# Attention into SwiGLU on one core: three more warming products and a paced one on TensorE, and v of batch 3 loaded in four steps from ScalarE's queue

## The chip, the cores and the metric

The kernel runs on one core of a Trainium2 chip. The metric is device microseconds of one execution. Before the change the median of 4 runs is 328.59 us (328.45 to 328.79).

## The reference

The inputs are q, k and v of shape (8 batches, 8 heads, 576 positions, 64), three weights and a gain of a feed-forward block, and the output is (4608, 512) float32. Each batch first goes through a linear attention with a positional weight, and every token then through a normalised SwiGLU block:

```
phi(x)  = concat(relu(x) * cos_w, relu(x) * sin_w)            # 64 -> 128 features
kv, z   = sum_s phi(k)[s] v[s]^T,  sum_s phi(k)[s]            # per head
attn    = phi(q) kv / (phi(q) . z + 1e-6)
x       = attn, heads side by side: (4608 tokens, 512)
xn      = x / sqrt(mean(x^2) + 1e-6) * rms_g
out     = (silu(xn w_gate) * (xn w_val)) w_out                # 512 -> 1536 -> 512
```

## The kernel before, in words

Every instruction is placed by hand; each engine runs its own list in order, and a semaphore makes one list wait for another. The names below are those of the code.

**A batch's attention.** `load_kv` and `load_q` (issued from SP, the sync engine) bring raw k, v and q into the tiles rk, rv and rq. There are two rk tiles, but only one rv and one rq. `k_phi` and `q_phi` (lines 209 on ScalarE, 211 on VectorE) make the cos half and the sin half of phi, in bf16, in kpm and qp. `v_cast` (line 265 on VectorE, 263 on ScalarE) makes vvm, v in bf16 with a column of ones; there are two vvm tiles. `kvz_pe` (72 small products, line 282, PSUM tile psA) sums phi(k) with v, first for the heads of the low half (pieces 0 and 1), then for the high half. `kvz_evac` copies the sum out. phi(q) is transposed by a DMA (`q_tr_dma`, line 246). `nd_pe` (line 310, psA again, for each of four groups j of 128 tokens) multiplies it with the sum; `nd_post` (lines 360 to 364, VectorE: rec, then xt) divides, and so frees psA for the next group; `x_sq` (line 375, ScalarE: scr) squares and sums; GpSimd takes the power -1/2 (rs, line 380); `x_norm` (line 387, VectorE: xn) scales; `x_tr_dma` (line 406) transposes into xnT. The last 64 positions of two batches share a fifth group (qtT, xnt_tail).

**A block of the feed-forward part.** Block b works on the first 512 positions of batch b, in slots. In slots 0 to 11 `gval_step` runs eight 128x512 products (line 426, into psG and psV, each with two banks used in turn), ScalarE takes the silu (line 435, sg) and VectorE multiplies (line 441, hT). In slots 12 to 15 `out_step` runs the twelve products of an output tile (line 446, psC), ScalarE copies it out (line 263, osb) and issues its store. Attention work of the next batch is hung into the slots: "pe" stands ahead of a slot's products, "pre" and "post" ahead of and behind its evacuation, and "mid" lies between the sixth and the seventh product of an output slot.

In block 1, attention of batch 2 is under way: the groups j = 0 to 3 have their `nd_pe` in slots 7, 9, 11 and in the middle of slot 12. Loads of batch 3 are issued there too:

```
n = (p, 13, 6 + p)[i] if b == 1 else 5 * i + p
at(b + n // 16, n % 16, "post", load_piece, which, nb, p)
```

For nb = 3 (b = 1) this puts piece p of k in slot p, all four pieces of v in slot 13, and piece p of q in slot 6 + p. In later batches the pieces of v are spread over slots 5 to 8. The two halves of v of batch 3 are cast by VectorE in block 2, in slot 1 (low) and slot 3 (high), behind that slot's `q_phi`; `kvz_pe` of batch 3 stands at the head of slot 4.

**Completion semaphores.** The loads, stores and transposes that SP and ScalarE issue share eight completion semaphores, which are handed out in turn in the order of the code over both queues. An instruction that issues a transfer waits until the transfer that had its semaphore before has landed, and what stands behind it on its engine waits as well.

**The opening.** While k of batch 0 arrives, TensorE runs products of a zero tile (`filler`, line 466). Behind twelve of them stand three `paced` products: each takes a slice of kpm as its weights, so it waits for that slice (`paced(7, 1)` for group 7 of the low half; `paced(0, 3)` and `paced(5, 3)` for groups of the high half), and each has one more filler behind it. Between the second and the third lies the product that spreads the gain over the partitions (line 487). Then follow the transposes of phi(q) (line 254).

Of the kernel before, what the change touches and what calls it, by code (L numbers as in the profile page):

```python
# [23 lines left out]
def kernel(  # L24
# [11 lines left out]
    nc = tc.nc  # L36
# [28 lines left out]
    NJ = 9  # L65
# [2 lines left out]

    raw = {}

    def load_kv(which, b, r0=0, r1=4, j0=0, j1=NJ):

        key = (which, b)
        if key not in raw:
            raw[key] = (two if which == "k" else one).tile(
                [P, 4, NJ * D], FP32, name=f"r{which}", tag=f"r{which}"
            )
        src = {"k": k, "v": v}[which]
        return nc.sync.dma_start(
            out=raw[key][:, r0:r1, j0 * D : j1 * D],  # L80
            in_=src[b, 2 * r0 : 2 * r1, :, :]
            .rearrange("h s d -> (h s d)")
            .rearrange("(r p n) -> p r n", p=P, n=NJ * D)[:, :, j0 * D : j1 * D],
        )

    def load_q(b, h0=0, h1=8):
        key = ("q", b)
        if key not in raw:
            raw[key] = one.tile([P, H, 4 * D], FP32, name="rq", tag="rq")
        return nc.sync.dma_start(  # L90
            out=raw[key][:, h0:h1, :],
            in_=q[b, h0:h1, 0:512, :].rearrange("h (p j) d -> p h (j d)", j=4),
        )

    def load_q_tail(b):
        t = four.tile([P, 4, D], FP32, name="rqt", tag="rqt")
        raw[("qt", b)] = t
        for g in range(2):
            d = nc.sync.dma_start(
                out=t[64 * g : 64 * g + 64, :, :],  # L100
                in_=q[b, 4 * g : 4 * g + 4, 512:576, :].rearrange("h s d -> s h d"),
            )
        return d

    def load_piece(which, b, p):
        if which != "q":
            load_kv(which, b, p, p + 1)
        elif p < 4:
            load_q(b, 2 * p, 2 * p + 2)
        else:  # L110
            load_q_tail(b)
# [12 lines left out]
    g_row = one.tile([1, DM], FP32, name="g_row")  # L124
    nc.scalar.dma_start(out=g_row[:, :], in_=moe_rms_g.rearrange("(o d) -> o d", o=1))
    load_kv("k", 0, *LOW)
    load_kv("k", 0, *HIGH)
    load_q_tokens(0, 0, 2)
    first_v = load_kv("v", 0, *LOW)
# [334 lines left out]
    def filler(n, bank):  # L464
        for _ in range(n):
            nc.tensor.matmul(bank, lhsT=warm[:, 0:P], rhs=warm[:, :], start=True, stop=True)


    idle = psO[1][:, :]
# [4 lines left out]
        for j in range(NJ):  # L474
            k_phi(A if rs is LOW or j < 6 else V, 0, j, 1, rs)

    def paced(j, r):

        nc.tensor.matmul(
            idle, lhsT=kp_main[0][:, j, r, :], rhs=warm[:, :], start=True, stop=True  # L480
        )
        filler(1, idle)

    filler(12, idle)
    paced(7, 1)
    paced(0, 3)
    nc.tensor.matmul(psG[0][:, :], lhsT=ones[:, :], rhs=g_row[:, :], start=True, stop=True)
    paced(5, 3)
    weight_dmas = []

    def gval_slice(c0, c1):
# [145 lines left out]
    def at(blk, n, where, f, *args):  # L637
        slots.setdefault((blk, n), none())[where].append((f, args))
# [26 lines left out]
    for nb in range(2, B):  # L665
        b = nb - 1
# [24 lines left out]
        for j in range(4):  # L691
            n = nds[j]
# [12 lines left out]
    for nb in range(3, B):  # L705

        b = nb - 2
        for i, which in enumerate(("k", "v", "q")):
            for p in range(5 if which == "q" else 4):
                n = (p, 13, 6 + p)[i] if b == 1 else 5 * i + p  # L710
                at(b + n // 16, n % 16, "post", load_piece, which, nb, p)

    def gval_step(blk, n, bank=None):
# [31 lines left out]
    for n in range(NNT - 2):  # L745
# [28 lines left out]
        if n in nd_at:  # L774
            j = nd_at[n]
# [52 lines left out]
    for (c0, c1), bank in (((0, 384), psC[1]), ((384, 512), psG[0])):  # L828
# [6 lines left out]
        for i in range(2):  # L835
            r0 = (6 + i) * S + 512
# [33 lines left out]
```

## Time and profile before

| | before |
|---|---|
| median of 4 runs | 328.59 us |
| the profiled execution: its time, its span | 328.45 us, 326.7 us |
| TensorE busy | 317.7 us (97%), 2441 products |
| VectorE, ScalarE, GpSimd busy | 185.5 us, 177.6 us, 32.0 us |
| granted TensorE clock, mean | 0.999 |
| bytes moved by DMA | 53.91 MB, mean 165 GB/s |

The span is the time from the first to the last instruction; 1.75 us of the run lie outside it. In the timelines a row gives its start, its duration, the engine, the line, the operation and how many were merged; the bracket at the end is the idle time of that engine just before it, and what ended it. PEld is the loading of weights on TensorE, ACT is ScalarE, DVE is VectorE, and a q behind an engine's name marks the issuing of a DMA on it.

### The profile page before, as it was taken

Reading aid. Unit: us, or ns where it says so; the run is one execution under the profiler, and the core shown is the slowest. Engines: PE = TensorE matmul, PEld = TensorE weight load, DVE = VectorE, ACT = ScalarE, POOL = GpSimd, SP = SyncE. Lnnn points to the kernel's source line nnn. Section 1 sums busy time; section 2 is a strip of 40 time slices with the busy share of each in tenths; the row PEclk is TensorE's granted clock in tenths of the full one; section 3 lists DMA queues with packets and bytes.
Section 4 is the critical chain, followed back from the end, with each engine's and each line's share of the span. In section 5 each row is a group of like instructions: output and inputs, shape, how many; then the busy total and the mean of one; then the engine's idle time right before and its main releaser. Section 6 shows DMA issues by size and latency. Waiting matters only on the chain.

```text
span 326.7 us, 6421 instructions
## 1 busy us (share of the span) xinstructions
PE 317.7 (97%) x2441; PEld 161.0 (49%) x2441; DVE 185.5 (57%) x412; ACT 177.6 (54%) x366; POOL 32.0 (10%) x67
## 2 busy tenths in 40 slices
PE   7999999999998999999999999999999999999994
PEld 2587465555444444554454445444544444444442
DVE  6875758777765766578257745773577133203310
ACT  6963865964774457644754476547644333223321
POOL 1660112001000100010001100110011000000000
PEclk9999999999999999999999999999999999999999
DMA  7999999999699665976597669957621400020014
GB/s 270 232 196 267 316 165 323 321 189 224 125 239 267 176 191 154 205 211 178 166 222 203 167 199 206 201 148 222 122 41 32 130 32 0 32 99 1 0 34 97
DMA packets 80338, 53.91 MB, mean 165 GB/s; under 512 B 51377, under 2 KB 67761, under 8 KB 80306
## 3 DMA queue, kind: packets, MB, share of 16 engines
q1 hardware_dynamic: 68752, 40.52, 50.6%
q0 software_dynamic: 6880, 4.72, 10.1%
q10 hardware_dynamic: 4674, 8.26, 7.7%
q8 instruction: 19, 0.31, 0.4%
q14 instruction: 13, 0.11, 0.1%
HBM read 37.75 MB, written 9.44 MB: 144 GB/s over the span
## 4 chain that ended last, share of the span: by engine, by line
PE 90%; DVE 4%; ACT 2%; DMA 1%; issue 1%; ACTq 0%; DVEq 0%
PE psG L426 26%; PE psC L446 26%; PE psV L426 26%; PE psA L282 3%; PE psA L310 2%; PE psG L446 1%; DVE kpm L211 1%; PE psG L565 1%; DMA rk<-in_k_dram 1%; PE psV L565 1%; PE psO L565 1%; DVE vvm L265 1%; DVE qp L211 1%; ACT kpm L209 1%; PE psC L830 1%
## 5 line engine op out<-in xcount | busy, mean ns | idle before, releaser
L441 DVE TENSOR_TENSOR hT<-psV,sg 128x512 bf16<-128x512 f32 x102 | 70.3, 689 | 93.1 <-PE psV L426 82.0
L435 ACT ACTIVATE sg<-psG 128x512 f32<-128x512 f32 x102 | 60.6, 594 | 64.9 <-PE psG L426 64.8
L426 PE MATMUL psG<-xnT,wg 128*128 128x512 bf16 (+1 forms) x368 | 92.9, 375 | 0.1
L426 PE MATMUL psV<-xnT,wv 128*128 128x512 bf16 (+1 forms) x368 | 92.7, 374 | 0.0
L446 PE MATMUL psC<-wo,hT 128*128 128x512 bf16 x396 | 89.5, 379 | 0.0
L426 PEld LDWEIGHTS <-wv 128*128 128x128 bf16 x416 | 40.7, 98 | 47.3
L446 PEld LDWEIGHTS <-hT 128*128 128x128 bf16 x420 | 40.2, 98 | 46.7
L426 PEld LDWEIGHTS <-wg 128*128 128x128 bf16 x416 | 38.5, 98 | 41.0 <-DVE xnT L265 0.4
L380 POOL TENSOR_TENSOR rs<-ms,mhalf 128x1 f32<-128x1 f32 x36 | 19.8, 549 | 200.9 <-ACT scr L375 200.9
L387 DVE SCALAR_TENSOR_TENSOR xn<-xt,rs,gb 128x512 bf16<-128x512 f32 x36 | 26.8, 745 | 19.3 <-POOL rs L380 19.3
L263 ACT COPY osb<-psC 128x512 f32<-128x512 f32 (+1 forms) x33 | 19.1, 579 | 32.5 <-PE psC L446 31.1
L375 ACT ACTIVATE scr<-xt 128x513 bf16<-128x513 f32 x36 | 22.8, 634 | 24.2 <-DVE xt L364 22.6
L209 ACT ACTIVATE kpm<-rk,tab 128x256 bf16<-128x256 f32 (+1 forms) x78 | 31.9, 476 | 7.0 <-ACT osb L263 5.4
L364 DVE TENSOR_TENSOR xt<-psA,rec 128x512 f32<-128x512 f32 x35 | 24.2, 691 | 1.2
L211 DVE TENSOR_SCALAR kpm<-rk,tab 128x256 bf16<-128x256 f32 (+1 forms) x84 | 22.2, 330 | 2.1 <-DMA rk<-in_k_dram 2.1
L209 ACT ACTIVATE qp<-rq,tab 128x512 bf16<-128x512 f32 x32 | 22.4, 713 | 0.0
L211 DVE TENSOR_SCALAR qp<-rq,tab 128x512 bf16<-128x512 f32 x32 | 15.1, 485 | 0.0
L310 PEld LDWEIGHTS <-qpT 128*128 128x128 bf16 x248 | 11.6, 98 | 6.7 <-issue 0.3
L310 PE MATMUL psA<-kvzs,qpT 128*128 128x65 bf16 x248 | 12.8, 194 | 0.2
L426 PE MATMUL psV<-xnt_tail,wv 128*128 128x512 bf16 x48 | 12.3, 379 | 0.0
L426 PE MATMUL psG<-xnt_tail,wg 128*128 128x512 bf16 x48 | 12.3, 379 | 0.0
L282 PEld LDWEIGHTS <-kpm 64*128 64x128 bf16 x576 | 9.9, 94 | 4.7 <-issue 4.0
(89 smaller groups left out, 167.5 us busy)
## 6 DMA issues: line engine op xcount, KB each, us to landing
out_dram<-osb ACTq DMA_DIRECT2D x28, 256.0 KB, 3.2
rv<-in_v_dram SPq DMA_DIRECT2D x21, 288.0 KB, 3.1
rk<-in_k_dram SPq DMA_DIRECT2D x20, 288.0 KB, 4.2
rq<-in_q_dram SPq DMA_DIRECT2D x20, 256.0 KB, 3.5
rk<-in_k_dram SPq DMA_DIRECT2D x2, 1152.0 KB, 8.8
rq<-in_q_dram SPq DMA_DIRECT2D x2, 1024.0 KB, 9.4
rv<-in_v_dram SPq DMA_DIRECT2D x3, 576.0 KB, 9.2
wo<-in_moe_w_out_dram POOLq DMA_DIRECT2D x4, 384.0 KB, 7.7
```

What stands on the lines that cost most here:

```text
L209: nc.scalar.activation(out=out_ap, in_=in_ap, func=AF.Relu, scale=scale)
L211: eng.tensor_scalar(out=out_ap, in0=in_ap, scalar1=scale, scalar2=0.0, op0=ALU.mult, op1=ALU.max)
L282: nc.tensor.matmul(banks[c][:, r * E : (r + 1) * E], lhsT=kp_main[b][lo : lo + 64, j, r, :], rhs=vvm[b % 2][lo : lo + 64, r, j, :], start= ...
L310: nc.tensor.matmul(o[:, g, i, :], lhsT=qpT[(b, 0)][:, h, j * P : (j + 1) * P], rhs=kvz_of(b, h), start=True, stop=True,)
L364: nc.vector.tensor_tensor(out=xt[:, 0:DM].rearrange("p (b h d) -> p b h d", b=2, d=D), in0=o[:, :, :, 0:D], in1=rec[:, :, :].unsqueeze(3). ...
L375: nc.scalar.activation(out=scr[:, :], in_=xt[:, 0 : DM + 1], func=AF.Square, scale=1.0 / math.sqrt(DM), accum_out=ms[:, :],)
L380: nc.gpsimd.tensor_tensor(out=rs[:, :], in0=ms[:, :], in1=mhalf[:, :], op=ALU.pow)
L387: nc.vector.scalar_tensor_tensor(out=xn[:, :], in0=x_of[(b, j)][:, 0:DM], scalar=rs_of[(b, j)][:, :], in1=gb[:, :], op0=ALU.mult, op1=ALU. ...
L426: nc.tensor.matmul(pst[bank][:, cols[0] : cols[1]], lhsT=w[:, t, n * P : (n + 1) * P], rhs=x[:, t, cols[0] : cols[1]], start=(t == 0), sto ...
L435: nc.scalar.activation(out=sg[:, :], in_=psG[bank][:, :], func=AF.Silu)
L441: nc.vector.tensor_tensor(out=hTs[blk][:, n, :], in0=psV[bank][:, :], in1=sg[:, :], op=ALU.mult)
L446: nc.tensor.matmul(bank, lhsT=hTs[blk][:, n, j * P : (j + 1) * P], rhs=wo[:, n, :], start=(n == 0), stop=(n == NNT - 1),)
```

## The change

There are two parts, in stages that lie some 70 us apart.

In the opening, fifteen fillers run in place of twelve; a fourth paced product, `paced(3, 1)`, which waits for group 3 of the low half of phi(k), stands ahead of the other three, with a filler behind it; and the filler behind the last paced product is gone. That is a net four products more.

In block 1, the four pieces of v of batch 3 are issued by ScalarE in place of SP, one each in slots 7, 8, 9 and 10, in place of all four in slot 13. The casts that read them stay where they are.

```
-    def load_kv(which, b, r0=0, r1=4, j0=0, j1=NJ):
+    def load_kv(which, b, r0=0, r1=4, j0=0, j1=NJ, eng=nc.sync):
...
-        return nc.sync.dma_start(
+        return eng.dma_start(
...
-            load_kv(which, b, p, p + 1)
+            eng = nc.scalar if (which, b) == ("v", 3) else nc.sync
+            load_kv(which, b, p, p + 1, eng=eng)
...
-    def paced(j, r):
+    def paced(j, r, more=1):
...
-        filler(1, idle)
+        filler(more, idle)
...
-    filler(12, idle)
+    filler(15, idle)
+    paced(3, 1)
     paced(7, 1)
     paced(0, 3)
     nc.tensor.matmul(psG[0][:, :], lhsT=ones[:, :], rhs=g_row[:, :], start=True, stop=True)
-    paced(5, 3)
+    paced(5, 3, 0)
...
-                n = (p, 13, 6 + p)[i] if b == 1 else 5 * i + p
+                n = (p, 7 + p, 6 + p)[i] if b == 1 else 5 * i + p
```

In the order in which the changed kernel is built, ScalarE's list in slots 7 to 11 of block 1 reads: x_sq (slot 7), **v piece 0**, phi of a tail, sg (slot 8), **v piece 1**, phi of a tail, sg (slot 9), x_sq (slot 9), **v piece 2**, sg (slot 10), **v piece 3**, sg (slot 11), x_sq (slot 11). VectorE's and GpSimd's lists have the same order as before. SP's list lacks the four v pieces and is otherwise in the same order. By the eight semaphores in turn, v piece 0 and v piece 1 each wait for a piece of k of batch 3, v piece 2 for piece 1 of q of batch 3, and v piece 3 for v piece 0.

## The prediction

> **What bounds the kernel now.** I read the page first (busy times, then the chain that ended last), then TensorE's waits, then the timelines of the two stages that the change touches.
>
> ```profile
> PE 317.7 (97%) x2441; PEld 161.0 (49%) x2441; DVE 185.5 (57%) x412; ACT 177.6 (54%) x366; POOL 32.0 (10%) x67
> PE 90%; DVE 4%; ACT 2%; DMA 1%; issue 1%; ACTq 0%; DVEq 0%
> ```
>
> TensorE is busy for 97% of the span and holds 90% of the last chain. A change gains only where TensorE idles, and whatever makes TensorE idle is lost one for one. Its waits:
>
> ```profile
> PE psA L282 <- DVE vvm L265: 1.2, 1, 1.2
> PE psO L466 <- DVE warm L145: 1.2, 1, 1.2
> PE psO L479 <- ACT kpm L209: 1.1, 1, 1.1
> PE psG L565 <- DVE xnT L265: 0.5, 1, 0.5
> PE psO L254 <- ACT qp L209: 0.3, 1, 0.3
> ```
>
> Two of these rows are near the change: 1.1 us ahead of the first paced product, and 1.2 us ahead of the high half of batch 3's sum, which waits for the cast of v.
>
> **Part 1, the opening: 0.** The weight loads, then the two products that matter:
>
> ```profile
> 4.58 0.15 PEld L466 LDWEIGHTS <-warm 128*128 128x128 bf16 x1 [0.28 <-issue]
> 4.98 0.31 PEld L466 LDWEIGHTS <-warm 128*128 128x128 bf16 x2 [0.25 <-issue]
> 6.92 0.10 PEld L479 LDWEIGHTS <-kpm 128*128 128x128 bf16 x1 [1.63 <-ACT kpm L209]
> 9.58 0.50 PEld L254 LDWEIGHTS <-qp 128*128 128x128 bf16 x9 [0.37 <-ACT qp L209]
> ```
>
> Up to 4.58 us a product takes 0.43 us; from 4.98 us on the spacing halves (7.73 - 7.51 = 0.22 between two later products). Twelve fillers end at 5.78 us. Five more products come ahead of `paced(7, 1)`: three fillers and the new pair, 5 x 0.22 = 1.1 us, against 1.14 us of idleness. The new paced product doesn't wait: ScalarE's fifteen phi steps take 4.49 us from 4.42, so its fourth ends at about 4.42 + 4 x 0.30 = 5.6 us, and VectorE's fourth of 21 (4.21 us from 4.44) at 5.2; TensorE gets there at about 6.2. `paced(7, 1)` therefore still starts at 6.92 us, when its own slice is there. The dropped filler frees 0.22 us ahead of the transposes, but these start at 9.58 us because phi of q ends on ScalarE at 8.82 + 0.70 = 9.52 us. So the work is covered from both sides: value 0. If the cover were gone, the four net products would cost 4 x 0.22 = 0.9 us; below nothing it can't go, since no later product in the opening waits for TensorE's own past: its waits of 0.3 and 0.5 us there are for ScalarE and VectorE. Nor can the pace improve: it is full from 5 us on (the granted clock reads 1.00 in the slow stretch too, so the spacing is the evidence).
>
> The Trainium skill speaks against this part ("TensorE: Matmul & The Clock Gate", Part 1): the half-rate start lasts until one whole free-running window of about 3.4 us was busy, so its end varies by run. By that rule an unlucky run would do all 17 products at 0.43 us and end them near 8.5 us, about 1.5 us late. The trace shows one run, with the change of pace at 5 us.
>
> The trace's own bound for a late change of pace: four runs lie within 0.34 us, so the pace can't wander much, and a rate change up to 6 us is absorbed (eleven of the 17 products done by then, six at 0.22 us end at 7.3 us, and the chain has 0.3 us to spare ahead of the transposes).
>
> **Part 2, v of batch 3: what it could gain is nothing.** The 1.2 us is not a wait for the transfer. In the chain of waits:
>
> ```profile
> 97.38 0.10 DVE hT L441
> ...
> 97.99 0.48 DVE qp L211
> 98.47 0.68 DVE vvm L265
> ...
> 99.19 0.76 PE psA L282 x36
> ```
>
> VectorE casts the high half only behind hT of slot 3, which waits for TensorE's last product of that slot, and behind a `q_phi`. There is no idle time between the three, and no wait for a DMA: the casts at 94.93 and 98.38 us start when VectorE is free. The order of VectorE's list is unchanged, so hT + phi + cast less the low half of the sum comes out at 1.2 us again. On SP, what stood behind the four v pieces is the tail's transpose at 92.18 us, and this waited for xn (91.40 + 0.75), not for the queue: 0.
>
> **What part 2 can cost** is on ScalarE. In the timelines (ScalarE, VectorE, TensorE; block 1, slots 9 to 12):
>
> ```profile
> 76.50 0.64 ACT L375 ACTIVATE scr<-xt 128x513 bf16<-128x513 f32 x1 [1.09 <-DVE xt L364]
> 77.13 0.58 ACT L435 ACTIVATE sg<-psG 128x512 f32<-128x512 f32 x1
> ```
>
> ```profile
> 77.74 0.69 DVE L441 TENSOR_TENSOR hT<-psV,sg 128x512 bf16<-128x512 f32 x1 [0.76 <-ACT sg L435]
> ...
> 79.44 0.69 DVE L364 TENSOR_TENSOR xt<-psA,rec 128x512 f32<-128x512 f32 x1
> ```
>
> ```profile
> 80.41 0.41 PE L310 MATMUL psA<-kvzs,qpT 128*128 128x65 bf16 x8
> ```
>
> This is a chain without slack. sg of slot 10 follows x_sq at once; hT waits for sg (0.76 us idle); xn, rec and xt run behind hT without a gap; xt frees psA at 79.44 + 0.69 = 80.13 us; and TensorE, in order, wants psA at 80.41 us. So 0.28 us, say 0.25 with the handover, is all that a delay D of sg may take; TensorE idles for D - 0.25.
>
> Pieces 0, 1 and 3 matter less: piece 1 stands ahead of an sg that waited 0.71 us, piece 3 behind the sg in question. Piece 0 delays hT of slot 8, and through VectorE's unbroken run from 73.74 to 76.99 us the x_sq of slot 9, by 0 to 0.43. Piece 2 stands directly between that x_sq and sg, and waits for q piece 1:
>
> ```profile
> 73.08 1.09 SPq L90 DMA_DIRECT2D rq<-in_q_dram  x2
> DMA to landing us min/median/max: 3.0/3.2/3.5
> ```
>
> (the second answer is of the tile rq in this stretch). q piece 1 is issued at about 73.65 us; landing by its row of 3.4 us: 77.05 us.
>
> Prices: issuing a v piece took 0.43 us (median of the four on SP near 87 us, 0.74 at most; stores of 256 KB on ScalarE 0.34 to 0.40): I take 0.43. No row shows whether ScalarE issues while its previous activation still runs, so both ends stand. Contention: v pieces now run beside q; one piece of 288 KB at the 287 GB/s of 73.3 to 74.2 us is 1.0 us.
> - Issue under the running activation, no contention: issue ends at 77.05 + 0.43 = 77.5, D = 0.4, stall 0.1.
> - Issue after it, no contention: piece 0 shifts x_sq to 76.93, with its accumulator read it ends near 77.65; issue to 78.1; D = 0.95, stall 0.7.
> - Contention, either way: q lands at 78.05, issue to 78.5; D = 1.35, stall 1.1.
>
> The first is one end; the other is a q piece that lands like the slowest v piece near 87 us (7.7 us): 81.35 + 0.43, D = 4.6, stall 4.4, which I hold for remote, since q rows here stay within 3.5. Counting the contended price once for each way of issuing, the four mean 0.75; I take **0.7 us**.
>
> By the Trainium skill ("DMA: Bandwidth & Descriptors", Issuing engines are not separate DMA queues) transfers from both queues interleave on the same 16 engines, so the second queue saves issue time alone; by it the contended price, 1.1 us, would stand.
>
> Downstream the shift runs along: x_sq, rs, xn and the transpose of group 3 (issued near 85.7 us, 4.1 us to landing: 89.8) move with TensorE, whose use is at 90.2 us.
>
> **Sum.** 0 + 0 + 0.7. The profiled execution took 328.45 us (span 326.7, 1.75 outside): 329.15. The median lies 0.14 us above it: **329.3 us**. A measurement of this kernel can't tell a difference within about 0.2%, 0.66 us, from none: that bound is 327.9 to 329.25.
>
> **The rivals.**
> - *Stall as reckoned*, 328.9 to 329.9 us: 0.5. Two thirds of it lie above 329.25.
> - *All of it hidden*: sg isn't held for more than 0.4 us; 328.4 to 328.9 us: 0.25. For it: ScalarE is 54% busy and idles 0.7 to 1.1 us before most sg. Against it: not before this one.
> - *q piece 1 lands late*, stall 1.5 to 3 us: 330.1 to 331.6 us, 0.1.
> - *The half-rate start lasts past 6 us*, and the longer warm-up delays the transposes: up to 0.9 us, 329.3 to 329.6 us with the stall small: 0.07.
> - *Faster*: the landing of v, not VectorE's order, holds the cast (the pieces took 5.4 to 7.7 us, so the last, issued at 88.7 us, landed as late as 96.4 us); landed earlier, it lets the cast go ahead and the wait of 1.2 us is gone: 327.4 us, 0.08. It decides only if the cast stood idle for the DMA, that is with a landing behind 98.4 us; in the trace VectorE has no such idle time.
>
> Slower: two thirds of 0.5, and 0.1, and most of 0.07, about 0.48; faster 0.08; the rest, 0.44, within the bound. The range leaves out the faster case and the late landing, 0.18: 328.3 to 330.0 us.
>
> **What would show it.** In the profile after: `paced(7, 1)` at 6.92 us with no idle time before it; the transposes at 9.58; ScalarE's third v issue at 77 to 78 us with sg behind it at 77.5 to 78.5; a new wait of TensorE's L310 for VectorE's xt near 80.4 us, of about 0.7; the 1.2 us ahead of L282 unchanged. No wait at L310 would prove the second case; an L282 wait that is gone would prove me wrong on VectorE's order; an L254 start after 9.6 us, on the opening.

## The result and the profile after

| | before | after |
|---|---|---|
| median of the runs shown with the result | 328.76 us (71 runs) | 329.98 us (45 runs) |
| ratio to before, 95% interval | | 1.0033 (1.0026 to 1.0039) |
| profiled execution: time, span | 328.45, 326.7 us | 329.88, 328.1 us |
| granted TensorE clock | 0.999 | 1.00 |

The change makes the kernel slower by 0.85 to 1.28 us. (Between the two profiled executions it is 1.43 us.) The page after, its busy times and the shares of the last chain by engine:

```profile
PE 318.5 (97%) x2445; PEld 161.4 (49%) x2445; DVE 185.8 (57%) x412; ACT 177.8 (54%) x366; POOL 31.9 (10%) x67
PE 87%; DMA 4%; DVE 3%; ACT 2%; issue 1%; SPq 1%; ACTq 0%; DVEq 0%
```

TensorE has its four products more. Its share of the last chain fell by 3 points, and transfers have more of it (DMA 4%, from 1%). About 1% is a load of q of batch 3, 4.37 us long, which nobody waited for before; most of the rest is a load of v in the opening, which landed later in this execution. Line numbers are one or two higher than before (L310 is L311, L435 is L436). TensorE's waits (total, times, longest) name the place:

```profile
PE psA L283 <- DVE vvm L266: 1.2, 1, 1.2
PE psO L467 <- DVE warm L146: 1.2, 1, 1.2
PE psA L311 <- DVE xt L365: 1.1, 1, 1.1
PE psG L567 <- DVE xnT L266: 0.5, 1, 0.5
PE psO L480 <- ACT kpm L210: 0.5, 1, 0.5
PE psO L255 <- ACT qp L210: 0.3, 1, 0.3
```

The third row is new. The 1.2 us ahead of the high half of batch 3's sum (first row) is still there. The wait ahead of the first paced products (L480) went from 1.1 to 0.5 us, but it was filled with products that nothing needs, so nothing was gained. ScalarE's timeline in slots 7 to 10 of block 1 shows where the third row comes from:

```profile
72.24 0.64 ACT L376 ACTIVATE scr<-xt 128x513 bf16<-128x513 f32 x1 [0.45 <-DVE xt L365]
72.37 0.38 ACTq L79 DMA_DIRECT2D rv<-in_v_dram  x1
...
76.64 0.64 ACT L376 ACTIVATE scr<-xt 128x513 bf16<-128x513 f32 x1 [1.09 <-DVE xt L365]
77.18 0.19 ACT L376 ACTIVATION_READ_ACCUMULATOR scr<-xt 128x1 f32 x1
78.37 0.36 ACTq L79 DMA_DIRECT2D rv<-in_v_dram  x1
78.78 0.60 ACT L436 ACTIVATE sg<-psG 128x512 f32<-128x512 f32 x1 [1.41 <-PE psG L427]
```

The third v piece is issued at 78.37 us, 1.00 us after the accumulator was read (77.18 + 0.19), and sg of slot 10, which followed at once before, starts behind it: 1.41 us of idleness. The bracket names psG as releaser, but psG had been full long before (its last product ended at 76.59 us): what came last is the issue, and what the issue waited for is piece 1 of q. The chain of waits in this stretch shows it (first block; "issue" is time without a wait that the profile shows). The second block is the answer for the tile rq, all four pieces of q:

```profile
73.98 4.37 DMA rq<-in_q_dram
78.35 0.02 issue
78.37 0.36 ACTq L79
```

```profile
DMA to landing us min/median/max: 4.2/4.3/5.3
```

Piece 1 of q, issued at 73.98 us, lands at 78.35 us, and the issue of v starts 0.02 us later. From there the chain runs through VectorE to TensorE:

```profile
79.40 0.69 DVE L442 TENSOR_TENSOR hT<-psV,sg 128x512 bf16<-128x512 f32 x1 [2.28 <-ACT sg L436]
...
81.10 0.69 DVE L365 TENSOR_TENSOR xt<-psA,rec 128x512 f32<-128x512 f32 x1
```

```profile
81.84 0.40 PE L311 MATMUL psA<-kvzs,qpT 128*128 128x65 bf16 x8 [1.13 <-DVE xt L365]
```

Before, TensorE needed 10.66 us from nd_pe of slot 7 (69.75) to nd_pe in the middle of slot 12 (80.41). After, it needs 11.95 us (69.89 to 81.84): 1.29 us more. From there to the first product of block 2 both need 9.79 us. The other 0.14 us were lost ahead of slot 7: in this execution v of batch 0 landed a little later. 1.29 + 0.14 = 1.43 us, the whole difference of the two profiles.

### The profile page after: what moved, and what is told of

It is laid out like the page before. It is cut to its first block, busy times and chain, and to the rows that moved or that the text cites. A ratio compares the mean times of both kernels' runs of the same rounds, so it can differ in the third digit from the quotient of the medians.

```text
span 328.1 us, 6430 instructions
## 1 busy us (share of the span) xinstructions
PE 318.5 (97%) x2445; PEld 161.4 (49%) x2445; DVE 185.8 (57%) x412; ACT 177.8 (54%) x366; POOL 31.9 (10%) x67
## 4 chain that ended last, share of the span: by engine, by line
PE 87%; DMA 4%; DVE 3%; ACT 2%; issue 1%; SPq 1%; ACTq 0%; DVEq 0%
PE psC L447 26%; PE psG L427 25%; PE psV L427 24%; PE psA L283 3%; DMA rv<-in_v_dram 2%; PE psA L311 2%; PE psG L447 1%; DMA rq<-in_q_dram 1%; PE psG L567 1%; PE psV L567 1%; PE psO L567 1%; ACT sg L436 1%; ACT kpm L210 1%; DVE xt L365 1%; PE psC L832 1%
## 5 line engine op out<-in xcount | busy, mean ns | idle before, releaser
L436 ACT ACTIVATE sg<-psG 128x512 f32<-128x512 f32 x102 | 60.6, 594 | 65.5 <-PE psG L427 65.4
L311 PEld LDWEIGHTS <-qpT 128*128 128x128 bf16 x248 | 11.6, 98 | 8.0 <-issue 1.7
L311 PE MATMUL psA<-kvzs,qpT 128*128 128x65 bf16 x248 | 12.8, 193 | 1.4 <-DVE xt L365 1.1
L283 PEld LDWEIGHTS <-kpm 64*128 64x128 bf16 x576 | 10.0, 95 | 4.9 <-issue 4.0
```

Of the source, the lines that this page charges most:

```text
L283: nc.tensor.matmul(banks[c][:, r * E : (r + 1) * E], lhsT=kp_main[b][lo : lo + 64, j, r, :], rhs=vvm[b % 2][lo : lo + 64, r, j, :], start= ...
L311: nc.tensor.matmul(o[:, g, i, :], lhsT=qpT[(b, 0)][:, h, j * P : (j + 1) * P], rhs=kvz_of(b, h), start=True, stop=True,)
L436: nc.scalar.activation(out=sg[:, :], in_=psG[bank][:, :], func=AF.Silu)
```

## The experiments

Two measures serve for all of them, both counted from nd_pe of slot 7 in the same execution, so that the opening drops out. D is how much later than before sg of slot 10 starts (before: 77.13 - 69.75 = 7.38 us). The loss is what the stretch from slot 7 to the middle of slot 12 exceeds 10.66 us by.

**The opening alone.** v stays with SP in slot 13.

```
-    filler(12, idle)
+    filler(15, idle)
+    paced(3, 1)
...
-    paced(5, 3)
+    paced(5, 3, 0)
```

> Only the opening is changed (fifteen fillers, the new paced product, no filler behind the last); v of batch 3 is loaded as before. Theory (the whole loss is the stall of TensorE at L310 behind ScalarE's third v issue): same time as before within 0.15% (0.5 us), the transposes of phi(q) at 9.6 us, no wait at L310. Rival (the opening costs something: the sum of phi(k) v of batch 0 began 0.14 us later in the profile after): 0.14 us slower or more, and that shift seen again near 10.8 us.

Measured: 328.83 us, ratio 0.9983 (0.9961 to 1.0005), loss 0.01 us. In the profiled execution the weight loads kept their slow spacing until 6.29 us, and still the transposes of phi(q) waited for ScalarE:

```profile
5.86 0.15 PEld L467 LDWEIGHTS <-warm 128*128 128x128 bf16 x1 [0.28 <-issue]
6.29 0.39 PEld L467 LDWEIGHTS <-warm 128*128 128x128 bf16 x2 [0.28 <-issue]
...
9.89 1.01 PEld L255 LDWEIGHTS <-qp 128*128 128x128 bf16 x16 [0.34 <-ACT qp L210]
```

So the opening costs nothing, and a late change of pace was absorbed: TensorE worked without a gap until the gain's product at 8.40 us, and was done in time. (ScalarE's phi of q was itself 0.3 us later here, as q of batch 0 landed at 9.1 us.) The rival's sign was there, and larger than expected: the sum of phi(k) v of batch 0 began at 11.37 us, 0.75 us later than before (10.62), and nd_pe of slot 7 as much later. It waited for the cast of v of batch 0, which landed 8.3 us after its issue, before 7.3. This isn't the opening's doing: with the old opening (next run) that landing took 8.6 us, with the new one (last run) 7.2.

**The load of v alone.** The opening stays as before; against the kernel after:

```
-    filler(15, idle)
-    paced(3, 1)
+    filler(12, idle)
...
-    paced(5, 3, 0)
+    paced(5, 3)
```

> Only the loading of v of batch 3 is changed. Theory: all of the change's loss, about +1.1 us (+0.33%), with a wait at L310 of about 1.1 us near 81.8 us. Rival (part of the loss is in the opening): +0.7 us or less.

Measured: 329.99 us, ratio 1.0023 (1.0005 to 1.0041), D 1.15 us, loss 0.94 us. The opening's part of the change is absent, and the wait is there. (The interval of the time alone, 0.2 to 1.3 us, doesn't tell the theory from the rival; the loss in the profile does.) TensorE's wait, then ScalarE's timeline:

```profile
PE psA L311 <- DVE xt L365: 0.8, 1, 0.8
```

```profile
78.96 0.36 ACTq L79 DMA_DIRECT2D rv<-in_v_dram  x1
79.37 0.60 ACT L436 ACTIVATE sg<-psG 128x512 f32<-128x512 f32 x1 [1.05 <-DMA rq<-in_q_dram]
```

Here the bracket of sg itself names the transfer of q that the issue ahead of it waited for. The experiments that follow, up to the cast, are edits of this kernel.

**The third piece behind sg.** As the run above, with piece 2 issued behind sg of slot 10: the same queue, number of issues and semaphores.

```
-                n = (p, 7 + p, 6 + p)[i] if b == 1 else 5 * i + p
+                n = (p, (7, 8, 10, 10)[p % 4], 6 + p)[i] if b == 1 else 5 * i + p
```

> As the v-only kernel, but piece 2 stands one slot later (slots 7, 8, 10, 10), behind sg of slot 10 and not ahead of it; its semaphore, the piece of q that it waits for, the queue, and the number of issues are the same. Theory (sg of slot 10 is held by the wait in front of it): the loss is gone, same as before within 0.15%; sg at 77.2 to 77.3 us, no wait at L310; the next sg may be late by about 0.7 us, which VectorE hides. Rival 1 (four issues on ScalarE cost their 0.36 us each, wherever they stand): still +1 us. Rival 2 (the early transfers disturb the other transfers): still +1 us.

Measured: 328.82 us, ratio 0.9996 (0.9978 to 1.0014), D 0.00, loss 0.00 us, and no wait at L311. ScalarE:

```profile
77.13 0.58 ACT L436 ACTIVATE sg<-psG 128x512 f32<-128x512 f32 x1
78.96 1.00 ACTq L79 DMA_DIRECT2D rv<-in_v_dram  x2
80.06 0.60 ACT L436 ACTIVATE sg<-psG 128x512 f32<-128x512 f32 x1 [2.35 <-PE psV L427]
```

The issue still waits (until 78.96 us), and now holds sg of slot 11 instead, which has time. The pieces of q still take 3.4 to 5.8 us to land. So neither the traffic nor the issuing on ScalarE is the loss: it is what stands behind the waiting issue.

**The third place with an older semaphore.** Slots (7, 8, 8, 9): the issue between the square of slot 9 and sg of slot 10 is now that of piece 3, which waits for v piece 0.

```
-                n = (p, 7 + p, 6 + p)[i] if b == 1 else 5 * i + p
+                n = (p, (7, 8, 8, 9)[p % 4], 6 + p)[i] if b == 1 else 5 * i + p
```

> As the v-only kernel, but the pieces stand in slots 7, 8, 8 and 9: there is again one issue between x_sq of slot 9 and sg of slot 10, at the very place that held sg, but by the turn of the semaphores it waits for v piece 0 (issued near 72.4 us), not for piece 1 of q (issued near 73.9 us). Theory: v piece 0 lands near 77 us, the issue itself runs while x_sq does, sg is held by 0.5 us at most, and TensorE by 0.3 us at most: +0.0 to +0.3 us. Rival (the issue itself, at that place, is what costs): still about +1 us, with sg near 78.5 us.

Measured: D 0.01, loss 0.00 us: an issue at the very same place costs nothing if its semaphore is free. It ran from 76.98 to 77.31 us under the square (76.93 to 77.56):

```profile
76.93 0.63 ACT L376 ACTIVATE scr<-xt 128x513 bf16<-128x513 f32 x1 [1.10 <-DVE xt L365]
76.98 0.33 ACTq L79 DMA_DIRECT2D rv<-in_v_dram  x1
...
77.56 0.58 ACT L436 ACTIVATE sg<-psG 128x512 f32<-128x512 f32 x1
```

But the time was 329.85 us, ratio 1.0033 (1.0010 to 1.0056), against my expectation, by another wait, 10 us on:

```profile
91.32 1.04 PE L427 MATMUL psG<-xnT,wg 128*128 128x512 bf16 x4 [0.54 <-DMA xnT<-xn]
```

The transposition of the last group took 5.2 us to land, against 4.1 before, where it had 0.4 us to spare (issued near 85.7, landed at 89.8, used at 90.2). The same kernel once more:

> The slots 7, 8, 8, 9 once more. If the late landing of the last transposition (5.2 us, wait of 0.54 us at 91.3 us) belongs to this arrangement, it is in this profile too and the ratio is again 1.002 to 1.004; if it was a chance of one execution, the landing is 4.1 us, the wait is gone, and the ratio is 1.000 to 1.001.

Measured: 330.08 us, ratio 1.0025 (1.0011 to 1.0040), landing 5.1 us, a wait of 0.42 us in the same place. It belongs to the arrangement and is no chance.

**v in slots 7 to 10 from SP.**

```
-            eng = nc.scalar if (which, b) == ("v", 3) else nc.sync
+            eng = nc.sync
```

> The change's v slots 7 to 10, but issued by SP; opening as before. Theory (the loss is sg of slot 10 held behind an issue on ScalarE's queue): ScalarE has no DMA issue between x_sq and sg, sg of slot 10 at about 77.1 us, no wait of TensorE for xt at the nd products of slot 12, ratio 1.000 within 0.001. Rival (the loss is the traffic beside q or the shared semaphores, whoever issues): ratio 1.003, stall of 1 us in slot 12. What could add a loss of its own: SP's transposes of xn move back by some 0.45 us each; those of groups 0 to 2 have time until 90.2 us, so 0.

Measured: 330.40 us, ratio 1.0034 (1.0020 to 1.0047). Half of the expectation held: D 0.00, loss 0.00 us. The ratio missed, by the late transposition again (5.4 us to land). ScalarE, then TensorE:

```profile
77.31 0.58 ACT L436 ACTIVATE sg<-psG 128x512 f32<-128x512 f32 x1
```

```profile
91.27 1.04 PE L427 MATMUL psG<-xnT,wg 128*128 128x512 bf16 x4 [0.73 <-DMA xnT<-xn]
```

**v in slots 7, 7, 8, 8 on ScalarE.** No issue stands between the square of slot 9 and sg of slot 10.

```
-                n = (p, 7 + p, 6 + p)[i] if b == 1 else 5 * i + p
+                n = (p, (7, 7, 8, 8)[p % 4], 6 + p)[i] if b == 1 else 5 * i + p
```

> Opening as before; v pieces on ScalarE's queue in slots 7, 7, 8, 8, so that none stands between the square of slot 9 and sg of slot 10 and none waits for a q piece. Theory for the loss of the change: no wait of TensorE for xt in slot 12. Left open by the slots 7, 8, 8, 9: whether the last transposition of xn lands late (5.1 to 5.4 us in three profiles, against 3.7 to 4.1 in the others). If its late landing comes with any early v load that doesn't delay slot 12, it is 5 us here too and the ratio 1.002 to 1.004; if it belongs to the issue under the square in slot 9 (which this kernel lacks), it is about 4 us and the ratio 1.000.

Measured: 329.03 us, ratio 1.0003 (0.9992 to 1.0014); the last transposition landed in 3.6 us, without a wait. D was 0.46 and the loss 0.24 us, this time without a wait for a transfer. Two issues stand one behind the other in slot 7. The first runs under the square, the second behind it, and the phi behind the second starts 0.44 us later than before (0.34 us of it idleness, named "issue"). ScalarE, then VectorE:

```profile
72.39 0.40 ACTq L79 DMA_DIRECT2D rv<-in_v_dram  x1
...
72.84 0.45 ACTq L79 DMA_DIRECT2D rv<-in_v_dram  x1
73.33 0.51 ACT L210 ACTIVATE qp<-rqt,tab 128x256 bf16<-128x256 f32 x1 [0.34 <-issue]
...
73.74 0.58 ACT L436 ACTIVATE sg<-psG 128x512 f32<-128x512 f32 x1
```

```profile
74.35 0.69 DVE L442 TENSOR_TENSOR hT<-psV,sg 128x512 bf16<-128x512 f32 x1 [1.25 <-ACT sg L436]
```

Counted from nd_pe of slot 7 (69.91 us), sg and hT of slot 8 are each 0.45 us later than before. VectorE works from there without a gap, so the square of slot 9 and sg of slot 10 come 0.46 us late. An issue that waits for nothing costs its time too, where no running activation covers it. (Piece 3 did wait, for a transposition of phi(q); but sg of slot 9 behind it was 0.19 us late, and its hT stood behind xt in any case.)

So an early load of v alone isn't what makes the last transposition late. What does, in two of the arrangements tried and not in the others, stays open.

**The cast one slot earlier.** If the 1.2 us at L283 are VectorE's order, they go when the cast of the high half moves ahead of hT of slot 3; this in the kernel before, with v still loaded in slot 13, and beside it with the early load of the third experiment.

```
-        at(vb, vn + 1 + (nb == 3), "post", v_cast, V, nb, *HIGH)
+        at(vb, vn + 1, "post", v_cast, V, nb, *HIGH)
```

> The kernel before with that one cast moved to slot 2, v still loaded by SP in slot 13 of block 1. The last v piece was issued at 88.7 us and landed at the latest 7.7 us later, 96.4 us, 0.3 us ahead of the earlier cast at 96.7. Theory: the early load isn't needed, gain 1.2 us, ratio 0.9963. Rival (the early load is what lets the cast move): the cast waits for a landing behind 96.7 us, in some executions at least, and the gain is smaller than that of the run with v early, by 0.3 us or more.

> v of batch 3 from ScalarE's queue in slots 7, 8, 10, 10 as in the run before, and VectorE's cast of its high half one slot earlier (behind hT of slot 2 of block 2 in place of slot 3). By my reading the 1.2 us wait ahead of the high half of batch 3's sum is VectorE's order: the cast then runs at about 96.7 to 97.5 us, the second 36 products follow the first at 97.97 without idle time, and the kernel gains 1.2 us on the kernel before: ratio 0.9963, about 327.5 us by a median of 328.75. Rival (hT of slot 3, now 0.1 to 0.7 us later, holds TensorE in its place): no gain or under 0.6 us.

Measured: alone, 327.46 us, ratio 0.9952 (0.9933 to 0.9970); with the early load, 327.83 us, ratio 0.9961 (0.9946 to 0.9977). The wait is gone in both. VectorE and TensorE of the first:

```profile
96.30 0.48 DVE L211 TENSOR_SCALAR qp<-rq,tab 128x512 bf16<-128x512 f32 x1
96.70 0.75 DVE L265 CAST vvm<-rv 128x1152 bf16<-128x1152 f32 x1
97.42 0.69 DVE L441 TENSOR_TENSOR hT<-psV,sg 128x512 bf16<-128x512 f32 x1
```

```profile
97.25 1.33 PE L282 MATMUL psA<-vvm,kpm 64*128 64x65 bf16 x72
98.51 1.04 PE L426 MATMUL psG<-xnT,wg 128*128 128x512 bf16 x3
```

The 72 products run as one stretch. The cast finds its v although that was loaded in slot 13, so the early load isn't needed for it. The 1.2 us of the removed wait lie within the interval of the gain (1.0 to 2.2 us).

**The opening with the cast.** Both edits, the opening's and the cast's, on the kernel before.

```
-    filler(12, idle)
+    filler(15, idle)
+    paced(3, 1)
...
-        at(vb, vn + 1 + (nb == 3), "post", v_cast, V, nb, *HIGH)
+        at(vb, vn + 1, "post", v_cast, V, nb, *HIGH)
```

> The opening of the change (fifteen fillers, paced(3, 1), no filler behind paced(5, 3)) and the cast moved to slot 2, v loaded by SP in slot 13. If the opening is worth nothing: the same as the cast alone, ratio 0.995 to 0.996 to the kernel before, about 327.5 us. If it is worth what the first run left open (ratio 0.9961 to 1.0005 of the opening alone, a gain of up to 1.2 us): ratio 0.993 or lower.

Measured: 327.39 us, ratio 0.9957 (0.9943 to 0.9970). It can't be told from the cast alone, so a gain of 1.2 us, which the first run's interval left open, isn't there; one of half a microsecond would not be seen here. In the profile the transposes of phi(q) start at 9.58 us, as before. The kernel before with one cast moved beats both kernels of this case; the opening may be had with it or not.

## Why the prediction was right, point by point

The case that I held likeliest came true in its mechanism: slower, by a new wait of TensorE at the nd products of slot 12. Its size was too small: 329.98 us lies within the range, at its upper end, but 0.08 us above the band of that case (328.9 to 329.9); I had named 329.3.

- **Part 1, 0 us: right.** `paced(7, 1)` started at 6.93 us and the transposes at 9.58, as predicted. One detail missed: there is idle time ahead of `paced(7, 1)`, 0.5 us, because the pace changed nearer 4.1 us in that execution. The rival of the late change of pace falls with the first experiment: it happened there (6.29 us, 5.1 us after the first weight load) and cost nothing. That four runs lie close together was no ground to say that the pace can't wander much: it does, and the stage absorbs it.
- **The Trainium skill on the pace** ("TensorE: Matmul & The Clock Gate", What's actually happening): the slow start ends after a busy window of about 3.4 us that runs free of the kernel. That its end varies is so: the slow spacing ended 2.5 us (opening and cast early), 2.9 (after) and 5.1 us (opening alone) after the first weight load. The shortest is below the page's window, and here the measurement decides.
- **Part 2, gain 0: right.** The 1.2 us ahead of the high half stayed with v landed early, and went with the cast moved and v late: it was VectorE's order.
- **Part 2, the path of the cost: right.** Issue, sg, hT, xt, nd_pe: each link is in the timelines above. The time that this chain may be late without loss was put at 0.25 us. Three profiles give it, as D less the loss: 1.51 - 1.29, 1.15 - 0.94 and 0.46 - 0.24, that is 0.21 to 0.22 us.
- **Part 2, the size: too small.** The stall was 1.29 us in the profile (1.13 of it in the wait's own row), where I took 0.7. The step that was off is the choice of D: I averaged four cases, half of them with q landing in its old time. It didn't: the pieces of q took 4.2 to 5.3 us in place of 3.0 to 3.5, and piece 1, which counts, 4.4 in place of 3.5. My contended case (landing 78.05, D 1.35, stall 1.1) was within 0.2 us of what happened; the rest is that q was issued 0.13 us later than before, counted from slot 7, and that 0.22 us were to spare in place of 0.25.
- **How ScalarE issues** was left open between two prices and is settled: the issue runs under the activation before it (72.37 within 72.24 to 72.88). A free issue would have cost nothing at this place, not 0.4; with the waiting one it makes no odds, as the square had long ended at 78.37. Piece 0 cost nothing either (sg of slot 8 starts 3.38 us after nd_pe of slot 7, as before); a second issue right behind it cost 0.45 us of delay (slots 7, 7, 8, 8).
- **The skill on the two queues** ("DMA: Bandwidth & Descriptors", Issuing engines are not separate DMA queues): by it the contended price was to be taken, since the transfers of both queues interleave on the same engines. The kernel after agrees (q from 3.2 to 4.3 us in the median, with v beside it), and that case was the nearest of the four. That the traffic alone lengthened q isn't shown: with the same v issued by SP in the same slots it took 3.4 us in the median. It says that a second queue saves issue time alone; here even that wasn't worth having, since SP's issue time held nobody up in the kernel before.
- **Downstream:** the transposition of the last group moved with the stall and landed in 3.7 us, without a wait, as reckoned. That it had only 0.4 us to spare was in my numbers, and I didn't price it: three profiles of other arrangements lost 0.4 to 0.7 us there.

## What to carry to other kernels

An issue of a transfer is an instruction of its engine, and if it waits, here for a shared completion semaphore, what stands behind it on that engine waits too (sg by 1.41 us): before moving an issue onto a compute engine, ask what it waits for and who stands behind it, and whether a running instruction covers its own 0.4 us. The same issue one instruction further on cost nothing. And before loading data earlier, see whether its reader was waiting for the data at all: here the wait was the order of the reader's engine, and moving the reader gained 0.5% (1.6 us, by the interval 1.0 to 2.2), with the load left where it was.

## What was not expected of the hardware

The transposition of the last group landed at the latest 4.1 us after its issue in nine of the profiles, and 5.1 to 5.4 us after it in three (v in slots 7, 8, 8, 9, twice, and v from SP); the timed runs of these were slower to match. None of the runs shows why. The pieces of q landed in 3.3 to 3.9 us (median 3.4) when SP issued v between them, but in 4.2 to 5.3 us when ScalarE did so from its own queue in the kernel after, with the same bytes; the other six profiles with v from ScalarE have medians of 4.3 to 5.1 us. The order of the issues differs too, so whether it is the queue or the order stays open.
